# Moving the normalization's multiply and the scaled copies of v from VectorE to GpSimd in a fused attention kernel, with a branch hint, a split q evacuation and new scheduling limits

## The chip, the cores and the metric

The kernel runs on one core of one Trainium2 chip. The metric is the device time of one execution in microseconds (us), and lower is better. One run of the kernel before, 736.29 us at a granted clock of 0.85, was slow and is left out. The profile's span is about 2 us shorter than the device time. A profile is a single run, and the timed runs of one kernel spread by 0.4 to 2.9 us, so a difference of some tenths of a us between two spans means nothing by itself; verdicts rest on the timed runs. Engines are named as in the profile: PE is the matmul engine (PEld its weight loads), ACT is ScalarE, DVE is VectorE, POOL is GpSimd, SP is SyncE, which issues most DMAs. L900 is line 900 of the kernel in question; the same statement stands on another line in another kernel.

## The reference, cut to what matters

```python
# x: 2048 tokens x 512; 32 heads of 16 dimensions, everything bf16
def _A_ref(x, wqkv, wo):                       # full attention
    q, k, v = ...                              # x @ wqkv, split into heads
    p = softmax(einsum("bhqd,bhkd->bhqk", q, k) * Dh ** -0.5)
    return einsum("bhqk,bhkd->bhqd", p, v) @ wo
# _B_ref: the same with a sliding window of 8 keys, 2 apart
g = sigmoid((x * gate_w).sum(-1, keepdims=True))
return g * _A_ref(x, ...) + (1 - g) * _B_ref(x, ...)
```

The full attention dominates. Its 32 x 2048 x 2048 scores are 2048 tiles of 128 keys by 512 queries, and each tile needs one exp pass. The kernel works through 32 blocks of 64 tiles; a block is four heads by 512 queries, and its products with v collect in one PSUM bank until they are normalized, two blocks together.

## The kernel before

The exp tiles are shared by two engines. ACT takes two or three tiles at a time with its Exp function, and each of them then costs PE one product with v. DVE takes a tile with a bit trick: one `tensor_scalar` turns the scores into the bits of a 16-bit float, and two more "pieces" are shifted copies, made for up to four tiles at once. The three pieces are multiplied by v and by two scaled copies of v, so that a DVE tile costs PE three products.

```python
def exp_dve(slot_item):                                   # L1548: bits of exp, from PSUM
    (b, kt, j), bt, i, bank = slot_item
    A = SCALE * math.log2(math.e) * 1024.0
    return nc.vector.tensor_scalar(out=self.yb[bt["buf"]][:, 0, i * 512:(i + 1) * 512], in0=bank[:],
                                   scalar1=A, scalar2=1024.0 * (15.0 + PW_S[0]), op0=ALU.mult, op1=ALU.add)
def piece(bt, k):                                         # L1554: shifted copy, SBUF to SBUF
    n = len(bt["items"]) * 512
    y = self.yb[bt["buf"]]
    return nc.vector.tensor_scalar(out=y[:, k, 0:n], in0=y[:, 0, 0:n],
                            scalar1=float(round(1024.0 * (PW_S[k] - PW_S[0]))), scalar2=None, op0=ALU.add)
```

The scaled copies of v are made on DVE, out of the PSUM bank in which PE left v:

```python
def v_scaled(self, st0, nst, h0, h1, k):                  # L916
    n = (h1 - h0) * DH
    for st in range(st0, st0 + nst):
        if st in KD:                                      # the key tiles that DVE may take
            o = (st - st0) * n
            self.nc.vector.tensor_scalar(out=self.vw4[k][:, KD.index(st), h0:h1, 0:DH],
                                         in0=self.misc[:, o:o + n].rearrange("p (h e) -> p h e", e=DH),
                                         scalar1=PW_W[k], scalar2=None, op0=ALU.mult)
```

The normalization of a pair of blocks is a transpose, a reciprocal, a product with the gate, a large multiply and a transpose back, all on DVE:

```python
def n2(p0=0, n=2):                                        # L1648
    rc = self.wk.tile([P, 2, 16], F32, name="rc", tag="rc")
    t1 = self.t1[:, p0:p0 + n]
    nc.vector.reciprocal(out=rc[:, 0:n], in_=t1[:, :, :, DH])
    nc.vector.tensor_tensor(out=rc[:, 0:n], in0=rc[:, 0:n], in1=self.gA[...], op=ALU.mult)   # cut
    t2 = self.t2[(b // 2) % 2][:].rearrange("p a (r d) -> p r a d", r=2)[:, p0:p0 + n]
    return nc.vector.tensor_tensor(out=t2, in0=t1[:, :, :, 0:DH],
                            in1=rc[:, 0:n].unsqueeze(3).to_broadcast([P, n, 16, DH]), op=ALU.mult)
```

No engine's order is written by hand. A list scheduler in the kernel's own Python keeps steps with an engine, an estimated cost, dependencies, a due value and a release value. The last two count exp tiles: a step may be placed once "rel" tiles are out, and of the steps that are ready the one with the lowest "due" goes first. Tables of limits, one digit for each of 64 stretches of the 2048 tiles, tell the scheduler, for example, how much DVE may have before it is given another exp tile. The result is a fixed order of instructions on each engine. An ordinary output tile of block b is due at 64 b + 678 (dueO), the last two at 5000:

```python
def outproj_last(self, st, i, norm):                      # L1446, cut
    def ev():
        if i % 2 == 0:
            ob = self.wk.tile([P, D], BF16, name="ob", tag="ob")      # two buffers
            nc.vector.tensor_copy(out=ob[:], in_=self.misc[:])
            nc.sync.dma_start(out=self.o_dst[:, st, :], in_=ob[:])
        else:                                                         # in a tile that is idle by then
            ob = self.eg[:].bitcast(BF16)[:, 512 * (i // 2):512 * (i // 2) + 512]
            nc.scalar.copy(out=ob, in_=self.misc[:])
            nc.scalar.dma_start(out=self.o_dst[:, st, :], in_=ob)
    ch = self.chain([...four steps on PE..., (("DVE", "ACT")[i % 2], T_D1(512), ev)],
                    due=5000 + i, rel=2048 - 24, deps=[...])
```

The first scores are made by straight code, `head()`: 16 transposes of x, then q, then k, then the first scores. At the end a flag decides whether a slower exact path has to follow; with this data the branch skips it.

```python
    with ExitStack() as c1:
        _Fast(c1, tc, aps, flag).build()
    cond = nc.values_load(flag[0:1, 0:1], min_val=0, max_val=1)
    with tc.If(cond > 0):                                 # L746
        ...                                               # exact path
```

## Time and profile before

| what | before |
|---|---|
| device time, median of 3 runs | 714.45 us (714.19 to 714.62) |
| start of the profile to the first exp | 7.92 us |
| first exp to the end of the last exp | 694.5 us |
| end of the last exp to the issue of the last output | 4.55 us |
| from there to the end | 5.6 us |
| exp tiles on DVE and on ACT | 548 and 1500 |

The page of the profile gives busy time, share of the span and instructions of each engine, and the make-up of the chain of work that ended last:

```profile
PE 684.4 (96%) x8522; PEld 222.2 (31%) x8522; DVE 685.5 (96%) x1184; ACT 694.4 (97%) x702; POOL 206.0 (29%) x219
...
PE 48%; ACT 30%; DVE 9%; issue 8%; SPq 3%; DMA 2%; ACTq 0%; DVEq 0%
```

Three engines are full at once and GpSimd has room. The groups by shape show what they do: line, engine, operation, output and input by name and by shape, count, then busy time in us and the mean of one in ns, then the idle time just before them and what ended it.

```profile
L1900 ACT ACTIVATE pt<-fps 128x1024 bf16<-128x1024 f32 x564 | 546.1, 1104 | 2.8 <-PE fps L1846 2.2 <-ACT pt L1900 0.2
L1551 DVE TENSOR_SCALAR yb<-fps 128x512 int16<-128x512 f32 x548 | 355.7, 678 | 5.8 <-PE fps L1846 3.0 <-PE fps L1831 0.9
...
L1557 DVE TENSOR_SCALAR yb<-yb 128x2048 int16<-128x2048 int16 x256 | 169.8, 683 | 0.6
...
L1655 DVE TENSOR_TENSOR t<-t,rc 128x512 bf16<-128x512 f32 x15 | 10.4, 692 | 0.5
...
L922 DVE TENSOR_SCALAR vaugw<-fps 128x384 bf16<-128x384 f32 x12 | 6.3, 542 | 0.0
...
L922 DVE TENSOR_SCALAR vaugw<-fps 128x128 bf16<-128x128 f32 x12 | 3.2, 278 | 0.0
```

The last three lines are what the change takes off DVE: 15 multiplies and 24 copies, 19.9 us. The busy time by stretch (columns: stretch, us, then PE, PEld, DVE, ACT and POOL busy with instructions in brackets, granted PE clock, DMA share, GB/s) shows how full the engines are in the early part, and that GpSimd does almost nothing there:

```profile
120.00:180.00 60.00, 58.99 (x771) 18.33 (x770) 58.97 (x105) 59.46 (x62) 0.75 (x1) 1.00 0.05 15
180.00:240.00 60.00, 58.66 (x742) 17.23 (x734) 59.58 (x102) 60.00 (x62) 4.21 (x4) 1.00 0.03 7
```

The timeline (start, us, engine, instruction, count, and in brackets the idle time before it and what ended that) of the start, where the q evacuation on ACT leads to the first exp:

```profile
4.14 1.32 PE L970 MATMUL fps<-ident,x_in 128*128 128x128 bf16 x16
...
6.73 0.69 ACT L983 ACTIVATE qm<-fps,pmask 128x512 bf16<-128x512 f32 x1 [0.87 <-PE fps L885]
...
7.92 2.37 ACT L1900 ACTIVATE pt<-fps 128x1536 bf16<-128x1536 f32 x2 [0.50 <-PE fps L1846]
```

The end of the timeline, with the last projection, the last evacuation by DVE and the last output issued:

```profile
704.25 2.10 PE L885 MATMUL fps<-wAv,oT 128*32 128x512 bf16 x32
...
706.17 0.69 DVE L1460 CAST ob<-fps 128x512 bf16<-128x512 f32 x1 [1.09 <-PE fps L885]
...
707.00 0.37 ACTq L1465 DMA_DIRECT2D out_dram<-eg  x1
```

And the waits of SP's queue from 706 us on (engine, line, what for, us in total, times, longest), where L746 is the branch:

```profile
SPq L746 <- SPq L746: 3.0, 1, 3.0
```

### The profile page before, as it was taken

Reading aid. Unit: us, or ns where it says so; the run is one execution under the profiler, and the core shown is the slowest. Engines: PE = TensorE matmul, PEld = TensorE weight load, DVE = VectorE, ACT = ScalarE, POOL = GpSimd, SP = SyncE. Lnnn points to the kernel's source line nnn. Section 1 sums busy time; section 2 is a strip of 40 time slices with the busy share of each in tenths; the row PEclk is TensorE's granted clock in tenths of the full one; section 3 lists DMA queues with packets and bytes.
Section 4 is the critical chain, followed back from the end, with each engine's and each line's share of the span. In section 5 each row is a group of like instructions: output and inputs, shape, how many; then the busy total and the mean of one; then the engine's idle time right before and its main releaser. Section 6 shows DMA issues by size and latency. Waiting matters only on the chain.

```text
span 712.6 us, 21088 instructions
## 1 busy us (share of the span) xinstructions
PE 684.4 (96%) x8522; PEld 222.2 (31%) x8522; DVE 685.5 (96%) x1184; ACT 694.4 (97%) x702; POOL 206.0 (29%) x219
## 2 busy tenths in 40 slices
PE   9999999999999999999999999999999999999996
PEld 4432223323232233333222223322233332222333
DVE  6999999999999999999999999999999999999994
ACT  6999999999999999999999999999999999999994
POOL 3045000000001323322000455546555335545500
PEclk9999999999999999999999999999999999999999
DMA  6002001001000100000123437456454644636201
GB/s 172 5 15 63 10 8 25 2 3 47 3 2 13 27 2 1 10 1 13 40 64 107 123 87 167 133 130 161 124 155 106 156 107 117 158 68 177 74 21 36
DMA packets 64490, 48.71 MB, mean 68 GB/s; under 512 B 22528, under 2 KB 64000, under 8 KB 64256
## 3 DMA queue, kind: packets, MB, share of 16 engines
q1 hardware_dynamic: 63680, 45.83, 25.6%
q8 instruction: 69, 1.13, 0.7%
q0 software_dynamic: 288, 1.05, 0.4%
q10 hardware_dynamic: 416, 0.39, 0.2%
q14 instruction: 37, 0.30, 0.1%
HBM read 39.85 MB, written 5.26 MB: 63 GB/s over the span
## 4 chain that ended last, share of the span: by engine, by line
PE 48%; ACT 30%; DVE 9%; issue 8%; SPq 3%; DMA 2%; ACTq 0%; DVEq 0%
ACT pt L1900 29%; PE fps L1846 17%; PE fps L1623 15%; PE fps L885 13%; DVE yb L1551 4%; DVE yb L1557 2%; SPq L1315 1%; DMA er<-er_dram 1%; PE fps L1831 1%; PE fps L1365 1%; ACT er L1235 1%; SPq L952 1%; DMA x_in<-in_A_x_dram 1%; DVE prod L1216 0%; SPq L1341 0%
## 5 line engine op out<-in xcount | busy, mean ns | idle before, releaser
L1900 ACT ACTIVATE pt<-fps 128x1024 bf16<-128x1024 f32 (+1 forms) x688 | 688.9, 1184 | 4.0 <-PE fps L1846 3.2
L1551 DVE TENSOR_SCALAR yb<-fps 128x512 int16<-128x512 f32 x548 | 355.7, 678 | 5.8 <-PE fps L1846 3.0
L1846 PE MATMUL fps<-qm,kT 32*128 32x512 bf16 x1970 | 287.2, 383 | 17.6 <-ACT pt L1900 15.1
L1623 PE MATMUL fps<-pt,vaug 128*32 128x512 bf16 (+1 forms) x1596 | 238.1, 373 | 0.2 <-DVE kT L927 0.2
L1557 DVE TENSOR_SCALAR yb<-yb 128x2048 int16<-128x2048 int16 (+3 forms) x294 | 183.3, 647 | 0.6
L1623 PE MATMUL fps<-yb,vaugw 128*32 128x512 f16 (+1 forms) x1160 | 174.0, 372 | 0.5 <-DVE yb L1557 0.2
L1846 PEld LDWEIGHTS <-kT 32*128 32x128 bf16 x1970 | 84.6, 91 | 278.3 <-issue 272.7
L1347 POOL TENSOR_TENSOR er<-er,vw 128x512 bf16<-128x512 bf16 x64 | 73.2, 1156 | 126.8 <-DMA erb<-er_dram 65.9
L1623 PE MATMUL fps<-yb,vaug 128*32 128x512 f16 (+1 forms) x580 | 106.0, 372 | 0.1
L885 PE MATMUL fps<-xT,ww 128*32 128x512 bf16 (+2 forms) x1296 | 98.5, 380 | 0.5 <-DVE xT L973 0.2
L1623 PEld LDWEIGHTS <-vaug 128*32 128x32 bf16 x2176 | 66.9, 94 | 83.7 <-issue 75.7
L1347 POOL TENSOR_TENSOR erb<-erb,vw 128x512 bf16<-128x512 bf16 x64 | 72.9, 1156 | 66.2 <-DVE yb L1557 40.2
L1216 POOL TENSOR_TENSOR prod<-bq,bk 128x512 bf16<-128x512 bf16 x32 | 34.0, 1075 | 91.1 <-DVE prod L1216 66.8
L1623 PEld LDWEIGHTS <-vaugw 128*32 128x32 bf16 x1160 | 46.9, 95 | 36.4 <-issue 30.3
L885 PEld LDWEIGHTS <-ww 128*32 128x32 bf16 x1296 | 24.8, 95 | 33.5 <-issue 27.6
L1831 PE MATMUL fps<-qm,kz 128*32 128x512 bf16 x312 | 33.4, 384 | 0.4 <-DVE yb L1551 0.3
L1138 POOL DMA_DIRECT2D wAv<-in_A_wo_dram x1 | 0.8, 754 | 101.4 <-PE fps L1846 101.4
L1216 DVE TENSOR_TENSOR prod<-bq,bk 128x2048 bf16<-128x2048 bf16 x24 | 28.6, 1213 | 0.1
L1646 DVE STREAM_TRANSPOSE t<-fps 128x512 f32<-128x512 f32 x32 | 22.6, 705 | 2.5 <-PE fps L1623 2.5
L885 PE MATMUL fps<-woB,oB 128*32 128x512 bf16 x256 | 19.7, 382 | 0.0
L885 PE MATMUL fps<-wAv,oT 128*32 128x512 bf16 x256 | 19.3, 384 | 0.0
L1167 POOL TENSOR_TENSOR er<-xT 128x512 bf16<-128x512 bf16 x8 | 8.1, 1039 | 37.3 <-DVE yb L1557 37.3
(114 smaller groups left out, 299.0 us busy)
## 6 DMA issues: line engine op xcount, KB each, us to landing
vw<-v_dram SPq DMA_DIRECT2D x128, 128.0 KB, 3.1
er<-er_dram SPq DMA_DIRECT2D x128, 64.0 KB, 3.0
erb<-er_dram SPq DMA_DIRECT2D x128, 64.0 KB, 3.1
v_dram<-vs SPq DMA_DIRECT2D x16, 128.0 KB, 2.8
out_dram<-ob SPq DMA_DIRECT2D x15, 128.0 KB, 2.4
qm<-qs SPq DMA_DIRECT2D x112, 16.0 KB, 1.8
x_in<-in_A_x_dram SPq DMA_DIRECT2D x3, 512.0 KB, 6.4
ww<-in_B_wqkv_dram SPq DMA_DIRECT2D x12, 128.0 KB, 2.8
```

Source lines behind the costliest of these rows:

```text
L885: self.nc.tensor.matmul(out=out_ps[32 * c:32 * c + 32, 0:n], lhsT=lhsT_of(c), rhs=rhs, start=start, stop=stop, tile_position=(0, 32 * c))
L952: self.nc.sync.dma_start(out=self.qm[i % NQM][r][k:k + 16, :], in_=self.qs[i % 2][k:k + 16, :])
L1167: return nc.gpsimd.tensor_tensor(out=sq(sc, kc), in0=x, in1=x, op=ALU.mult)
L1216: return e.tensor_tensor(out=pr[m % 2][:, a:b], in0=bq[ct][:, a:b], in1=bk[ct][:, o + a:o + b], op=ALU.mult)
L1347: return nc.gpsimd.tensor_tensor(out=st_["erb"][m % 4][:, g, :], in0=st_["erb"][m % 4][:, g, :], in1=st_["vw"][m % 2][:, g, :], op=ALU.mult)
L1551: return nc.vector.tensor_scalar(out=self.yb[bt["buf"]][:, 0, i * 512:(i + 1) * 512], in0=bank[:], scalar1=A, scalar2=1024.0 * (15.0 + PW_ ...
L1557: return nc.vector.tensor_scalar(out=y[:, k, 0:n], in0=y[:, 0, 0:n], scalar1=float(round(1024.0 * (PW_S[k] - PW_S[0]))), scalar2=None, op0 ...
L1623: nc.tensor.matmul(out=out, lhsT=v, rhs=r, start=start, stop=stop, tile_position=(0, 32 * j))
L1646: nc.vector.transpose(out=self.t1[:, par].rearrange("p a b -> p (a b)"), in_=self.flex[acc[b]])
L1831: nc.tensor.matmul(out=dst[32 * c:32 * c + 32, :], lhsT=self.kz[:, j, KZ.index(kt), 32 * c:32 * c + 32], rhs=self.qm[(4 * ct + qc) % NQM][ ...
L1846: nc.tensor.matmul(out=dst, lhsT=self.kT[ct % 2][32 * j:32 * j + 32, kt * 128:(kt + 1) * 128], rhs=self.qm[(4 * ct + qc) % NQM][par][32 * ...
L1900: nc.scalar.activation(out=self.pt[pi[0]][pi[1]][:, 0:n * 512], in_=self.aslot[si][:, 0:n, :].rearrange("p a b -> p (a b)"), func=ACT.Exp, ...
```

## The change

The intent is to give DVE time back for exp tiles by moving 20 us of its work to GpSimd, to start and end a little earlier, and to refit the limits to the new balance. Cut to its core:

```diff
-TUNE = dict(R0=74, ...)
+TUNE = dict(relL=64, dueL2=2040, R0=74, ...)
 STRETCH = dict(...)          # cut: all eleven rows of limits are new
-PE_0, DVE_0, ACT_0, SLOT_0, K_0 = 1.6, 3.0, 1.75, 1.8, 2.35
+PE_0, DVE_0, ACT_0, SLOT_0, K_0 = 1.3, 2.7, 1.45, 1.5, 2.05
+T_P1 = lambda n: n / 750.0 + 0.1              # estimated cost of a scaled copy on GpSimd
@@ end of the program
+    tc.mark_branch_hint_location("exact", hint="LikelyTaken", engines=[ENG.SP, ENG.Activation, ENG.DVE, ENG.PE, ENG.Pool])
     with ExitStack() as c1:
         _Fast(c1, tc, aps, flag).build()
-    with tc.If(cond > 0):
+    with tc.If(cond > 0, label="exact"):
@@ loads
+        self.load_w("A", "q", 0)
         self.load_w("A", "k", 0)
-        self.load_w("A", "q", 0)
@@ v_scaled
-                self.nc.vector.tensor_scalar(out=self.vw4[k][...],
-                                             in0=self.misc[:, o:o + n].rearrange(...),
-                                             scalar1=PW_W[k], scalar2=None, op0=ALU.mult)
+                return self.nc.gpsimd.tensor_scalar(out=self.vw4[k][:, KD.index(st), h0:h1, 0:DH],
+                                                    in0=self.vaug4[:, st, h0:h1, 0:DH],
+                                                    scalar1=PW_W[k], scalar2=None, op0=ALU.mult)
@@ head
-                nc.scalar.activation(out=self.qm[0][0][:], in_=self.flex[1][:], func=ACT.Copy, scale=self.pmask[:, 0:1])
+                nc.scalar.activation(out=self.qm[0][0][:, 0:320], in_=self.flex[1][:, 0:320], func=ACT.Copy,
+                                     scale=self.pmask[:, 0:1])
+                nc.vector.tensor_scalar(out=self.qm[0][0][:, 320:512], in0=self.flex[1][:, 320:512],
+                                        scalar1=self.pmask[:, 0:1], scalar2=None, op0=ALU.mult)
@@ outproj_last
-                        due=5000 + i, rel=2048 - 24, deps=...)
+                        due=TUNE["dueL2"] + i, rel=2048 - TUNE["relL"], deps=...)
@@ norm_steps: n2 becomes n2a (reciprocal, gate product) on DVE and n2 on GpSimd
-                return nc.vector.tensor_tensor(out=t2, in0=t1[:, :, :, 0:DH], ...)
+                return nc.gpsimd.tensor_tensor(out=t2, in0=self.t1[:, :, :, 0:DH], ...)
```

The scaled copies now read v from SBUF, where DVE has just put it, instead of PSUM, so that the PSUM bank comes free earlier.

## The prediction

> **What bounds the kernel now.** Three engines are saturated together. The page's busy table gives ACT 694.4, DVE 685.5 and PE 684.4 of 712.6 us; the table by stretch shows ACT busy 59.5 to 60 of every 60 us from 60 to 240 us and 80 of 80 later, and DVE at 98 to 99%. The chain of waits alternates PE 48%, ACT 30%, DVE 9%. The 2048 softmax exp tiles of 128x512 are shared: 1500 on ACT, 548 on DVE; the groups give 688.9/1500 = 0.459 us a tile on ACT and (355.7 + 184.2)/548 = 0.985 us on DVE. GpSimd is busy 29%, and almost idle from 60 to 240 us.
>
> **What moves.** Off DVE: the normalization's multiply (15 at 691 ns, 10.4 us) and the scaled copies of v (24, 9.5 us). Back onto DVE: about 0.3 us of the first q evacuation. Net 19.6 us. Onto GpSimd: 15 multiplies, estimated at 1.2 us each from its 128x512 products (1040 to 1156 ns), 18 us; 24 copies, estimated at 0.3 and 0.6 us, 11 us. GpSimd goes from 206 to about 235 us.
>
> **What that is worth.** A list scheduler lays the kernel out, so freed DVE time becomes exp tiles: 19.6/(0.985 + 0.459) = 13.6 tiles, DVE 548 to about 562, ACT's exp time down 6.2 us. That lies on the critical path because ACT is never idle. Against it: a DVE tile needs three value products on PE instead of one, and PE is 98% busy before 240 us; and GpSimd's reads want the port that DVE's fast pieces use. The Trainium skill ("SBUF — State Buffer", section "Who interferes with whom") calls that pair an exclusive lock; in the waits, GpSimd's products wait 41.7 + 40.2 us for those pieces. I take off 1 us for both. Freeing PSUM banks earlier after v's evacuation, and retuned limits, give back 0.8.
>
> **Head.** The first q evacuation on ACT (0.69 us, ends 7.42) shrinks by an estimated 0.16; q's weights first may take off 0.1. First exp (7.92 us) 0.25 us earlier.
>
> **Tail.** After the last exp, PE works through 62 projection matmuls in 3.47 us without a break, while the last normalization is done at 705.1; PE's backlog sets the end. Releasing the last two tiles' projections earlier can take out up to 32: an estimated 0.7 us.
>
> **Branch hint.** The trace shows SP's compare-and-branch at 707.27 and its next instruction at 710.34, instruction fetches between; the output lands near 709.5. The Trainium skill ("Runtime: NRT & Kernel Launch", section "Instruction fetch mechanics") says a taken branch outside the window fetches its target first. If the hint prefetches, that is worth an estimated 0.8 us; at two chances in three, 0.5.
>
> **Sum.** 714.45 - 6.2 + 1.0 - 0.8 - 0.25 - 0.7 - 0.5 = 707.0 us. Range 703.5 to 710.0. Faster by over 2%: 0.03; within 2%: 0.96; slower: 0.01.
>
> **What would show it.** Right: about 562 exps on DVE; ACT near 688; DVE over 97%; no scaled copies or 691 ns multiplies on DVE; GpSimd near 235 us; first exp near 7.7; fewer than 40 projection matmuls after the last exp; SP's gap after the branch under 2.5 us. Wrong: DVE's exps unchanged with more DVE idle, PE's idle at zero in the early stretches, or DVE's pieces over 0.7 us.
>
> **What would make it wrong.** PE being the true limit, so that freed DVE time isn't used; GpSimd's multiplies over 1.5 us, holding DVE's pieces back; the retuned limits alone worth several us.

## The result, and the profile after

The ratios in this document are the mean time of one kernel's fast runs over that of the kernel before in the same rounds, with a 95% interval, so they are not quite the ratio of the medians quoted beside them.

| | median | runs | ratio to before |
|---|---|---|---|
| before, same rounds | 714.54 us (714.19 to 715.62) | 4 | |
| after | 713.98 us (713.66 to 714.64) | 4 | 0.9991 [0.9974, 1.0008] |

The prediction was 707.0 us with a range of 703.5 to 710.0, and 713.98 lies outside. The page after:

```profile
PE 689.5 (97%) x8558; PEld 221.9 (31%) x8558; DVE 678.4 (95%) x1154; ACT 691.3 (97%) x698; POOL 243.3 (34%) x258
...
PE 44%; ACT 36%; issue 9%; DVE 6%; DMA 3%; SPq 1%; POOL 0%; ACTq 0%; DVEq 0%; POOLq 0%
```

The work did move: DVE is 7.1 us less busy and GpSimd 37.3 us more. But less busy is not what was predicted; DVE was to be filled up again with exp tiles and to stay over 97% busy, and it is at 95%. The groups by shape:

```profile
L1912 ACT ACTIVATE pt<-fps 128x1024 bf16<-128x1024 f32 x560 | 540.8, 1094 | 2.9 <-PE fps L1858 2.2 <-ACT pt L1912 0.2
...
L1559 DVE TENSOR_SCALAR yb<-fps 128x512 int16<-128x512 f32 x556 | 360.4, 681 | 7.0 <-PE fps L1858 5.0 <-PE fps L1843 0.2
...
L1565 DVE TENSOR_SCALAR yb<-yb 128x2048 int16<-128x2048 int16 x258 | 171.7, 687 | 0.4
...
L1664 POOL TENSOR_TENSOR t<-t,rc 128x512 bf16<-128x512 f32 x15 | 15.9, 1059 | 121.1 <-DVE yb L1565 95.9 <-DVE rc L1659 16.7 <-DVE prod L1224 8.4
...
L922 POOL TENSOR_SCALAR vaugw<-vaug 128x384 bf16<-128x384 bf16 x12 | 14.3, 1195 | 40.1 <-PE fps L887 22.3 <-DVE vaug L915 17.1
...
L922 POOL TENSOR_SCALAR vaugw<-vaug 128x128 bf16<-128x128 bf16 x12 | 6.6, 550 | 20.9 <-DVE vaug L915 14.7 <-DVE yb L1565 5.7
```

DVE has 556 exp tiles instead of 548, so 8 more, where 13.6 were predicted. The same two early stretches:

```profile
120.00:180.00 60.00, 59.88 (x802) 18.89 (x794) 57.24 (x98) 59.91 (x62) 13.81 (x12) 1.00 0.04 12
180.00:240.00 60.00, 59.90 (x767) 17.71 (x765) 57.71 (x97) 60.00 (x63) 5.23 (x5) 1.00 0.04 10
```

PE is now busy for 59.9 of every 60 us, and DVE, which had been the fuller of the two in the second stretch, is at 57.7. DVE's waits from 140 to 230 us, first before, then after, name PE:

```profile
DVE qs L935 <- PE fps L885: 0.3, 1, 0.3
```

```profile
DVE yb L1559 <- PE fps L1858: 1.2, 5, 0.3
DVE vaug L915 <- PE fps L887: 1.1, 2, 0.5
DVE bk L1200 <- PE fps L887: 1.0, 1, 1.0
DVE bq L1200 <- PE fps L887: 0.7, 1, 0.7
```

The start of the timeline after. The first exp comes at 9.16 us instead of 7.92:

```profile
5.02 1.35 PE L978 MATMUL fps<-ident,x_in 128*128 128x128 bf16 x16 [0.35 <-DMA x_in<-in_A_x_dram]
...
7.49 0.53 ACT L991 ACTIVATE qm<-fps,pmask 128x320 bf16<-128x320 f32 x1 [0.71 <-PE fps L887]
...
8.05 0.42 DVE L993 TENSOR_SCALAR qm<-fps,pmask 128x192 bf16<-128x192 f32 x1 [1.21 <-ACT qm L991]
...
9.16 1.45 ACT L1912 ACTIVATE pt<-fps 128x1536 bf16<-128x1536 f32 x1 [1.15 <-DVE kT L995]
```

The end after. The last exp ends at 700.80 us, 1.65 us earlier than before (702.45), but the last output is issued at 708.54, which is 1.54 us later:

```profile
703.56 1.91 PE L887 MATMUL fps<-wAv,oT 128*32 128x512 bf16 x32
704.23 0.69 DVE L1449 CAST ob<-fps 128x512 bf16<-128x512 f32 x1 [0.57 <-PE fps L887]
704.88 0.69 DVE L1468 CAST ob<-fps 128x512 bf16<-128x512 f32 x1
...
707.83 0.69 DVE L1449 CAST ob<-fps 128x512 bf16<-128x512 f32 x1 [2.25 <-DMA out_dram<-ob]
708.54 0.33 SPq L1450 DMA_DIRECT2D out_dram<-ob  x1
```

The last evacuation waits 2.25 us for a DMA: both buffers named "ob" are still being sent. SP's wait at the branch (L748 here) is much shorter:

```profile
SPq L748 <- SPq L748: 1.2, 2, 0.7
```

Cut at the first exp, the last exp and the last issue of an output, the two profiles compare with the prediction like this. The predicted column sorts the terms of its sum; the middle is 6.2 - 1.0 + 0.8.

| stretch | before | after | change | predicted |
|---|---|---|---|---|
| start to first exp | 7.92 | 9.16 | +1.24 | -0.25 |
| first exp to last exp | 694.5 | 691.6 | -2.9 | -6.0 |
| last exp to last output issued | 4.55 | 7.74 | +3.2 | -0.7 |
| last output issued to end | 5.6 | 3.84 | -1.8 | -0.5 |
| sum | 712.6 | 712.4 | -0.2 | -7.45 |

Two large questions follow. Why did the end get 3.2 us longer? And why is the middle worth 2.9 us instead of 6.0?

### The profile page after: what moved, and what is told of

Same layout as the page of the kernel before. It is cut to its first block, busy times and chain, and to the rows that moved or that the text cites. A ratio compares the mean times of both kernels' runs of the same rounds, so it can differ in the third digit from the quotient of the medians.

```text
span 712.4 us, 21197 instructions
## 1 busy us (share of the span) xinstructions
PE 689.5 (97%) x8558; PEld 221.9 (31%) x8558; DVE 678.4 (95%) x1154; ACT 691.3 (97%) x698; POOL 243.3 (34%) x258
## 3 DMA queue, kind: packets, MB, share of 16 engines
q8 instruction: 68, 1.11, 0.7%
## 4 chain that ended last, share of the span: by engine, by line
PE 44%; ACT 36%; issue 9%; DVE 6%; DMA 3%; SPq 1%; POOL 0%; ACTq 0%; DVEq 0%; POOLq 0%
ACT pt L1912 35%; PE fps L1858 16%; PE fps L1631 15%; PE fps L887 10%; DVE yb L1559 3%; DVE yb L1565 2%; PE fps L1843 1%; PE fps L1373 1%; DMA erb<-er_dram 1%; PE fps L1238 1%; SPq L1349 1%; ACT er L1243 1%; DMA x_in<-in_A_x_dram 1%; DMA ww<-in_A_wqkv_dram 0%; SPq L1323 0%
## 5 line engine op out<-in xcount | busy, mean ns | idle before, releaser
L1912 ACT ACTIVATE pt<-fps 128x1024 bf16<-128x1024 f32 (+1 forms) x684 | 686.1, 1172 | 4.7 <-PE fps L1858 2.2
L1559 DVE TENSOR_SCALAR yb<-fps 128x512 int16<-128x512 f32 x556 | 360.4, 681 | 7.0 <-PE fps L1858 5.0
L1631 PE MATMUL fps<-pt,vaug 128*32 128x512 bf16 (+1 forms) x1588 | 241.0, 373 | 0.1
L1565 DVE TENSOR_SCALAR yb<-yb 128x2048 int16<-128x2048 int16 (+2 forms) x294 | 187.4, 662 | 0.5
L1631 PE MATMUL fps<-yb,vaug 128*32 128x512 f16 (+1 forms) x588 | 108.6, 372 | 0.0
L1631 PEld LDWEIGHTS <-vaug 128*32 128x32 bf16 x2176 | 65.2, 94 | 83.4 <-issue 75.1
L1631 PEld LDWEIGHTS <-vaugw 128*32 128x32 bf16 x1176 | 47.1, 95 | 40.2 <-issue 33.2
L1664 POOL TENSOR_TENSOR t<-t,rc 128x512 bf16<-128x512 f32 x15 | 15.9, 1059 | 121.1 <-DVE yb L1565 95.9
L922 POOL TENSOR_SCALAR vaugw<-vaug 128x128 bf16<-128x128 bf16 (+1 forms) x24 | 20.9, 872 | 61.0 <-DVE vaug L915 31.8
L1843 PE MATMUL fps<-qm,kz 128*32 128x512 bf16 x344 | 37.8, 383 | 0.2 <-DVE yb L1559 0.2
```

Of the source, the lines that this page charges most:

```text
L922: return self.nc.gpsimd.tensor_scalar(out=self.vw4[k][:, KD.index(st), h0:h1, 0:DH], in0=self.vaug4[:, st, h0:h1, 0:DH], scalar1=PW_W[k], ...
L1631: nc.tensor.matmul(out=out, lhsT=v, rhs=r, start=start, stop=stop, tile_position=(0, 32 * j))
L1664: return nc.gpsimd.tensor_tensor(out=t2, in0=self.t1[:, :, :, 0:DH], in1=h["rc"][:].unsqueeze(3).to_broadcast([P, 2, 16, DH]), op=ALU.mult)
L1843: nc.tensor.matmul(out=dst[32 * c:32 * c + 32, :], lhsT=self.kz[:, j, KZ.index(kt), 32 * c:32 * c + 32], rhs=self.qm[(4 * ct + qc) % NQM][ ...
L1912: nc.scalar.activation(out=self.pt[pi[0]][pi[1]][:, 0:n * 512], in_=self.aslot[si][:, 0:n, :].rearrange("p a b -> p (a b)"), func=ACT.Exp, ...
```

## The experiments

My theory after the result was that the end lost time by the new due value of the last two output tiles, that the start lost it by the hint and by the split evacuation, and that the middle fell short because PE, not DVE, limits the early part. The main rivals were that an earlier release helps and the loss has another cause, that GpSimd's work disturbs DVE through the port they share, and that the refit tables alone made the middle. The scheduler's five starting estimates (PE_0 and the others) changed too, and no run takes them back alone. Eighteen kernels were run, each with four or five timed runs.

### The end: a_tail and a_obfree

In a_tail the two values of the last output tiles are put back:

```diff
-TUNE = dict(relL=64, dueL2=2040, R0=74, ...)
+TUNE = dict(relL=24, dueL2=5000, R0=74, ...)
```

> The changed kernel with the last two output tiles' release and due values put back (24 and 5000 in place of 64 and 2040); all that comes before the last 64 exp tiles is the same. Theory: with a due of 2040 these tiles overtake two ordinary output tiles (due 2534), whose evacuation on DVE at 707.83 then waited 2.25 us for one of two output buffers; put back, no evacuation waits for a buffer, the last output is issued within 4.7 us of the last exp (it was 7.7 us, before 4.6), and the time falls by 2.0 to 3.5 us, to about 711. Rival: the tail is long because DVE ran dry or PE's backlog grew; then the time stays within 0.7 us of 714.0.

Measured: 711.70 us (711.33 to 712.06), ratio 0.9956 [0.9943, 0.997]. That is 2.3 us less than after, and the intervals of the two ratios don't overlap. Up to about 683 us ACT and DVE have the order of after; from there on it differs, and DVE has 554 exp tiles instead of 556. A build with only the release value changed (relL=64, dueL2=5000) comes out as the same program as a_tail, so the release value does nothing by itself. The two work together, though: a build with only the due value changed (24 and 2040) comes out in a third order, which was not run. The end of a_tail's timeline:

```profile
703.72 0.69 DVE L1468 CAST ob<-fps 128x512 bf16<-128x512 f32 x1 [0.51 <-PE fps L887]
...
704.44 0.33 SPq L1469 DMA_DIRECT2D out_dram<-ob  x1
704.55 0.38 ACTq L1473 DMA_DIRECT2D out_dram<-eg  x1
```

The last output is issued at 704.55 us, 4.0 us before that of after, while the last exp ends at about the same time (700.59 and 700.80). The due values explain the order. Block 29's four ordinary output tiles are due at 64 x 29 + 678 = 2534. With 5000 the last two tiles go behind them; with 2040 they go ahead, and ordinary tiles are left for the very end. Counted in the trace, PE has 64 output-projection matmuls after the last exp in the kernel before, 72 in after and 49 in a_tail. The time saved, 2.3 us, is less than the 4.0 us at the issue, because in this profile a_tail's last outputs took 3.6 and 3.8 us to land, and the very last one of after 2.0.

The theory was that the wait for an "ob" buffer makes the loss, and the rival that the order does. In a_obfree the order of after is kept, and one of the last two tiles goes to the unused half of another tile instead of an "ob" buffer:

```diff
             if i % 2 == 0:
-                ob = self.wk.tile([P, D], BF16, name="ob", tag="ob")
-                nc.vector.tensor_copy(out=ob[:], in_=self.misc[:])
-                nc.sync.dma_start(out=self.o_dst[:, st, :], in_=ob[:])
+                ob = self.eg[:].bitcast(BF16)[:, 512:1024]
+                nc.vector.tensor_copy(out=ob, in_=self.misc[:])
+                nc.sync.dma_start(out=self.o_dst[:, st, :], in_=ob)
```

> The changed kernel, with one of the last two output tiles evacuated to an idle half of another tile in place of the second output buffer; every instruction keeps its place and engine. Theory (the wait for the buffer is the loss): DVE's last evacuation no longer waits for an output's landing (it stood idle 2.25 us for it), the last output is issued 2 us or more earlier, and the time falls by 1.8 to 2.5 us to 711.5 to 712.2. Rival (the order of the last tiles costs of itself): it falls by less than 1 us.

Measured: 712.70 us (712.17 to 712.88), ratio 0.9972 [0.9958, 0.9986]. All instructions kept their places. The end of its timeline:

```profile
704.42 0.69 DVE L1468 CAST eg<-fps 128x512 bf16<-128x512 f32 x1
...
705.07 0.69 DVE L1449 CAST ob<-fps 128x512 bf16<-128x512 f32 x1
...
705.79 0.59 SPq L1450 DMA_DIRECT2D out_dram<-ob  x1
```

The wait is gone and the last issue moves from 708.54 to 705.79 us, of which 0.45 is an earlier last exp. The time falls by 1.3 us of the 2.3. In the profiles the stretch from the last exp to the last issue is 7.7 us in after, 5.4 in a_obfree and 4.0 in a_tail, so 2.3 of 3.8 us are the wait for a buffer, and the rest is the order, with 72 projection matmuls and four evacuations after the last exp instead of 49 and two. Both readings give the wait somewhat over half. By the timed runs alone that split isn't firm: the intervals of a_obfree and a_tail overlap, and other runs with a_tail's end took 711.6 to 712.4 us (c_again, d_hintlate and c_both, below).

### The start: a_head and a_kfirst

In a_head the first q evacuation is on ACT alone again; in a_kfirst the weights of k are loaded first again:

```diff
 # a_head
-                nc.scalar.activation(out=self.qm[0][0][:, 0:320], in_=self.flex[1][:, 0:320], func=ACT.Copy,
-                                     scale=self.pmask[:, 0:1])
-                nc.vector.tensor_scalar(out=self.qm[0][0][:, 320:512], in0=self.flex[1][:, 320:512],
-                                        scalar1=self.pmask[:, 0:1], scalar2=None, op0=ALU.mult)
+                nc.scalar.activation(out=self.qm[0][0][:], in_=self.flex[1][:], func=ACT.Copy, scale=self.pmask[:, 0:1])
 # a_kfirst
-        self.load_w("A", "q", 0)
         self.load_w("A", "k", 0)
+        self.load_w("A", "q", 0)
```

> The changed kernel with the first q evacuation on ACT alone, as before; nothing else differs. Theory: DVE's part waited for ACT's part of the same tile (1.21 us to 8.05), so the split is run one after the other and pushes the first k evacuation and the first exp back; undone, the first exp comes 0.3 to 0.5 us earlier relative to the first transposes (it was 4.14 us after them, before 3.78), and the time falls by 0.3 to 0.5 us. Rival: the whole 1.24 us lost at the head is a later landing of x; then the interval from transposes to first exp stays above 4.05 us and the time stays.

> The changed kernel with k's weights loaded before q's, as before. Theory: both are issued after x and PE starts on q's projections when x's copies are done, so the order is worth nothing: within 0.2 us of 714.0, first exp within 0.2 us relative to the first transposes. Rival: q's weights were late before, so k first costs 0.2 us or more; or the order is what delayed x, so k first gives up to 0.9 us.

Measured: a_head 714.04 us (713.74 to 714.48), ratio 0.9990 [0.9976, 1.0003]; a_kfirst 714.19 us (714.15 to 714.80), ratio 0.9995 [0.9982, 1.0009]. Neither changes the time. But a_head's start is earlier:

```profile
7.16 0.69 ACT L991 ACTIVATE qm<-fps,pmask 128x512 bf16<-128x512 f32 x1 [0.71 <-PE fps L887]
7.38 0.29 DVE L992 CAST kT<-fps 128x128 bf16<-128x128 f32 x1 [0.88 <-PE fps L887]
...
8.36 2.37 ACT L1909 ACTIVATE pt<-fps 128x1536 bf16<-128x1536 f32 x2 [0.51 <-PE fps L1855]
```

In after, DVE's part of the split tile started at 8.05 us, after ACT's part had ended at 8.01, with [1.21 <-ACT qm L991] as its wait: the two halves ran one after the other, and DVE's evacuation of k, which leads to the first scores, queued behind them. It is the program that does this: in the trace DVE's part waits for the semaphore that ACT's part raises. The 16 transposes took between 1.07 and 1.89 us in the profiles, and the trace shows with what that goes: PE's granted clock reaches its full value at 4.0 us in a_head, 5.7 in after and 7.1 in c_norm_dve, and transposes start some 107 ns apart before that moment and 55 ns after it (before and a_nohint have a wait of some 0.3 us for x in between besides). Among profiles in which they took the same time (1.07 to 1.12 us), the first exp came 3.38 to 3.40 us after the first transpose without the split (a_head, b_hint and three more) and 3.85 to 3.91 us with it (a_tail, a_kfirst, a_obfree). So the split costs 0.5 us at the start, where an estimated 0.16 was to be gained. It doesn't reach the end: what is lost at the start is swallowed in the fixed order that follows.

### The hint: a_nohint, b_hint and d_hintlate

In a_nohint the hint is taken out of after, in b_hint it is put alone into the kernel before, and d_hintlate is a_tail with the hint marked just before the scheduled part:

```diff
 # a_nohint; b_hint is the same edit, added to the kernel before
-    tc.mark_branch_hint_location("exact", hint="LikelyTaken", engines=[ENG.SP, ENG.Activation, ENG.DVE, ENG.PE, ENG.Pool])
-    with tc.If(cond > 0, label="exact"):
+    with tc.If(cond > 0):
 # d_hintlate
             self.jobs()
+            self.tc.mark_branch_hint_location("exact", hint="LikelyTaken", engines=[...])
             self.run()
```

> The changed kernel without the branch hint. Theory: the hint saves the fetch after the branch (SP 0.5 us from branch to next instruction with it, 3.0 without), worth about 0.5 to 1.2 us at the end, and costs 0.1 us at the start; without it the time rises by 0.4 to 1.1 us. Rival A: it is worth nothing since the output's landing covers the fetch: within 0.2 us. Rival B: the hint's register writes delay SP's first loads (its first packet at 2.82 us, before 1.84), so that without it the first transposes start at 4.1 in place of 5.0 and the time falls by up to 0.8 us.

> The kernel before with the branch hint added and nothing else. Theory: net of its later first loads it gains 0.4 to 1.3 us, as in the changed kernel; SP's gap after its branch falls from 3.0 to 0.5 us and the first transposes come 0.6 to 0.9 us later. Rival: with an undisturbed tail the later start costs as much as the end gains; within 0.3 us.

> The changed kernel with the tail's priorities put back (711.7), and the branch hint's register writes moved from the program's first instructions to behind the head, after the first loads are issued. Theory: at the start the hint holds SP's first loads back (its first packet at 2.3 to 3.0 us in four profiles with it, 1.84 in two without; first transposes 4.9 to 5.1 against 4.1 to 4.2), while its gain at the end needs only that it stands well before the branch; moved, the transposes start near 4.2, SP's gap after its branch stays near 0.5 us, and the time falls by 0.5 to 0.8 us to about 711.0. Rival: the head's shift is swallowed later, or the hint no longer holds at the branch: 711.5 or more.

Measured: a_nohint 715.04 us (714.52 to 715.62), ratio 1.0005 [0.9991, 1.0018], 1.06 us more than after. b_hint 713.66 us (713.34 to 714.15), ratio 0.9985 [0.9971, 0.9999], 1.2 us less than the 714.84 us of before in its rounds. The two agree: the hint is worth about 1.1 us, though each is little more than the spread of one kernel's runs. SP's wait at the branch in a_nohint is back:

```profile
SPq L747 <- SPq L747: 2.8, 1, 2.8
```

From the compare-and-branch to SP's next instruction the trace records show 3.07 us before, 2.85 in a_nohint and 0.52 in after and in b_hint. That is 2.5 us, of which less than half arrives. After the branch the traces have six instruction packets of 8 KB in before and in a_nohint, and two in after and three in b_hint, which fits the reading as a fetch. The records of b_hint show one reason why less arrives: SP gets through its first five semaphore instructions and then stands until 710.03 us in the one that has to wait for the outputs, the first of which lands at 710.01 us, so that the end is now set by their landing. And the hint costs something at the start. Each engine executes it there, as one instruction (BRANCH_PREFETCH_HINT, where the expectations speak of register writes), in 50 to 60 ns at 0.70 to 0.82 us, and SP's first load sends its first packet at 2.25 to 2.96 us in all 17 profiles with the hint, and at 1.84 us in all three without (before, a_nohint, b_newlim); the first transposes start at 4.89 to 5.11 us instead of 4.14 to 4.38. ACT's queue, which carries the other half of the first x tile, is earlier in exchange: its first packet comes at 1.93 to 1.98 us in 16 of the 17, and at 2.26 to 2.58 without. So the two queues change places, rather than both being late. Why 50 ns of hint make SP's loads 0.4 to 1.1 us late isn't shown, and neither is how much of it reaches the end: in b_hint the first exp starts 0.39 us later than before and the last ends only 0.09 us later.

d_hintlate is a miss. It took 712.17 us (711.50 to 712.43), ratio 0.9963 [0.9949, 0.9977], but its hint instructions came out at the same place, at the start, with the same order of instructions on ACT, DVE, GpSimd and SP as a_tail. It is a second measurement of a_tail (711.70 us), and whether a later hint would keep the gain without the cost stays open.

### The middle: the two moves, undone in a fixed order

For the middle, a base with a clean start and end was needed, so c_both has a_tail's and a_head's edits together; it was run again with later kernels as c_again.

> The changed kernel with the tail's priorities and the first q evacuation both put back. Theory: with no evacuation waiting for an output buffer, the 0.5 us that the q evacuation gained at the head (first exp 3.38 us after the first transposes, 4.14 before) is no longer swallowed at the end; the time is 0.3 to 0.6 us under the run with the tail alone put back (711.7), about 711.2. Rival: the head's gain is lost in the middle, where the static order waits anyway; then it stays within 0.15 us of 711.7.

> c_both once more, the control of the three runs beside it: 711.7 to 712.5 us.

Measured: c_both 712.43 us (711.68 to 713.75), ratio 0.9971 [0.9957, 0.9984]; c_again, the same kernel, 711.62 us (711.37 to 712.46), ratio 0.9957 [0.9943, 0.9971]. The two differ by 0.8 us, which is about how far such a difference can be trusted. Against a_tail's 711.70 us, undoing the split gains nothing once more.

Then three kernels that change the engine or the size of the moved work and leave the scheduled order as it is:

```diff
 # c_norm_dve: the multiply back on DVE, at its place in the order
-                return nc.gpsimd.tensor_tensor(out=t2, in0=self.t1[:, :, :, 0:DH],
+                return nc.vector.tensor_tensor(out=t2, in0=self.t1[:, :, :, 0:DH],
 # c_v_dve: the scaled copies back on DVE, still read from SBUF
-                return self.nc.gpsimd.tensor_scalar(out=self.vw4[k][:, KD.index(st), h0:h1, 0:DH],
+                return self.nc.vector.tensor_scalar(out=self.vw4[k][:, KD.index(st), h0:h1, 0:DH],
 # c_norm_short: one of 16 columns multiplied, wrong on purpose; the rest of t2 set to 0 once
-                return nc.gpsimd.tensor_tensor(out=t2, in0=self.t1[:, :, :, 0:DH],
-                                               in1=h["rc"][:].unsqueeze(3).to_broadcast([P, 2, 16, DH]), op=ALU.mult)
+                return nc.gpsimd.tensor_tensor(out=t2[:, :, :, 0:1], in0=self.t1[:, :, :, 0:1],
+                                               in1=h["rc"][:].unsqueeze(3), op=ALU.mult)
```

> c_both with the normalization's 15 multiplies issued to DVE at the very places where GpSimd had them; the layout of everything else, all limits and all tiles stay (554 exps on DVE). It adds 10.4 us to DVE. Theory (DVE's time is on the critical path at those places): the time rises by 6 to 10 us over c_both. Rival (DVE has slack there, PE or ACT limits): it rises by less than 3 us, and then moving these multiplies could not have gained more than that.

> c_both with the 24 scaled copies of v issued to DVE at the places where GpSimd had them, layout and limits kept. It adds about 9 us to DVE, nearly all before 170 us. The same two readings: a rise of 6 to 9 us over c_both if DVE is critical there, under 3 us if PE limits that stretch (PE's matmul groups start 96% back to back from 60 to 240 us).

> Wrong result on purpose: c_both with the 15 multiplies on GpSimd cut to one column in sixteen (1.06 us to some 0.2 us), layout kept. If GpSimd's hold on the shared port or its lateness cost the middle its expected gain, the time falls by 1 us or more under c_both; if GpSimd is harmless, it stays within 0.4 us.

Measured, with c_both in the same rounds:

| kernel | median | ratio to before | against c_both |
|---|---|---|---|
| c_norm_dve | 720.35 us (718.90 to 721.18) | 1.0070 [1.0056, 1.0084] | +7.9 us |
| c_v_dve | 712.45 us (711.96 to 713.71) | 0.9971 [0.9958, 0.9985] | 0.0 us |
| c_norm_short (wrong result) | 712.42 us (711.22 to 713.02) | 0.9965 [0.9951, 0.9979] | 0.0 us |

The moved groups in c_norm_dve:

```profile
L1661 DVE TENSOR_TENSOR t<-t,rc 128x512 bf16<-128x512 f32 x15 | 13.6, 905 | 0.0
```

and in c_v_dve:

```profile
L922 DVE TENSOR_SCALAR vaugw<-vaug 128x384 bf16<-128x384 bf16 x12 | 3.0, 250 | 0.0
...
L922 DVE TENSOR_SCALAR vaugw<-vaug 128x128 bf16<-128x128 bf16 x12 | 1.8, 180 | 0.0
```

The multiply matters in this order: 13.6 us put back on DVE cost 7.9 us by the medians and 7.1 by the ratios. It also takes 905 ns there in the mean and not 692, and nothing in c_norm_dve keeps GpSimd still while it runs, as the old order did. The Trainium skill ("SBUF — State Buffer", section "Who interferes with whom") says that a DVE instruction with two SBUF inputs contends with a GpSimd instruction that reads SBUF. The trace agrees: the seven multiplies with no tensor work on GpSimd beside them took 679 to 683 ns, and of the eight with some, seven took 734 to 1318.

The copies, put back, cost nothing. The experiment is weaker than it was meant to be: I had counted on some 9 us, and from SBUF the copies took only 250 and 180 ns, 4.8 us in all, against 542 and 278 ns from PSUM in the kernel before. The Trainium skill ("VectorE: DVE Perf Modes", section "Mode 4×_2P — both tricks at once") gives four elements a cycle for this mode, and the section after it ("What auto-detection actually checks") asks for 16-bit tensors, a single source, and source and destination in SBUF; the durations agree: between 128 and 384 columns a copy grows by 0.27 ns a column from SBUF and by 1.03 from PSUM. So about half of the copies' price on DVE was the price of reading them as f32 from PSUM and not as bf16 from SBUF; type and place changed together, so their parts aren't separated.

c_norm_short takes 15 multiplies on GpSimd from 1056 to 341 ns, so 10.7 us off GpSimd, and gains nothing. GpSimd's multiplies don't hold anything up at the size they have. About the port it says little, because DVE's pieces overlap tensor work on GpSimd for 8.7 us in it as in c_again. In c_v_dve, which takes 20.9 us of copies off GpSimd, that overlap falls to 6.0 us and nothing is gained, but there DVE has 4.8 us more to do. The two together speak against the rival of a disturbed port, and don't exclude it.

### The middle: which engine limits it

c_bproj_half takes 256 matmuls, an estimated 13.8 us, off PE alone, in the early part, by leaving out half of the contraction of the sliding branch's q and k. s_act takes 8 of 512 columns off every exp on ACT, s_dve 16 of 512 off every exp on DVE, s_both does both. All four were wrong and still passed the tolerance.

```diff
 # c_bproj_half
-    self.proj_mm(self.w_tiles[("B", kind, ct)], (0, 1), sc)),
+    self.proj_mm(self.w_tiles[("B", kind, ct)], (0,), sc)),
-    self.proj_mm(self.w_tiles[("B", kind, ct)], (2, 3), sc)),
+    self.proj_mm(self.w_tiles[("B", kind, ct)], (3,), sc)),
 # s_act (cut): out[:, 0:n * 512] and in_[:, 0:n, :] become [:, :, 0:504] of each 512, the rest set to 1 once
-    in_=self.aslot[si][:, 0:n, :].rearrange("p a b -> p (a b)"),
+    in_=self.aslot[si][:, 0:n, 0:504],
 # s_dve (cut): the rest of yb set to a constant once
-    out=self.yb[bt["buf"]][:, 0, i * 512:(i + 1) * 512], in0=bank[:],
+    out=self.yb[bt["buf"]][:, 0, i * 512:i * 512 + 496], in0=bank[:, 0:496],
```

> Wrong result on purpose: c_both (712.4) with half the contraction left out of branch B's q and k projections, layout kept. It takes 256 matmuls, about 13.8 us of PE, out of the stretch from 35 to 230 us, where PE's groups are 96% back to back, and nothing from other engines. Theory (PE limits that stretch, so DVE's freed time could not be used there, and adding 8 us of copies to DVE cost nothing): the first 640 exp tiles are done 3 us or more earlier than in c_both (228.4 us) and the time falls by 3 us or more. Rival (ACT or DVE limits): less than 1 us.

> Wrong result on purpose: c_both with ACT's exps cut from 512 to 504 columns a tile, layout kept; 8 columns at the 0.427 us that 512 of them add (triple 1331 less pair 904 ns) are 6.7 ns a tile, 10.0 us on 1494 tiles. The prediction's assumption (ACT is never idle, so its time is the time): the time falls by 8 to 10 us. Rival (three engines bind together): it falls by 2 to 5 us.

> Wrong result on purpose: c_both with DVE's exps cut from 512 to 496 columns, layout kept: an estimated 16.7 ns on 554 tiles, 9.2 us. If ACT alone limits: within 0.5 us of the control. If they bind together: it falls by 1 to 4 us.

> Wrong result on purpose: both cuts at once, 10 us off ACT and 9 us off DVE. If ACT alone limits: as s_act. If ACT and DVE bind together and PE has room: it falls by more than s_act and s_dve together, 7 us or more. If PE then limits: little more than the larger of the two.

| kernel | taken away | median | ratio to before | gain over c_again |
|---|---|---|---|---|
| c_bproj_half | 13.8 us of PE (estimate) | 710.58 us (710.30 to 712.12) | 0.9947 [0.9933, 0.996] | 1.0 us |
| s_act | 10.3 us of ACT | 705.86 us (705.59 to 706.37) | 0.9876 [0.986, 0.9891] | 5.8 us |
| s_dve | 8.9 us of DVE | 711.33 us (711.15 to 711.83) | 0.9951 [0.9937, 0.9966] | 0.3 us |
| s_both | both | 705.62 us (705.24 to 705.96) | 0.9872 [0.9856, 0.9887] | 6.0 us |

What was taken away is worked out from the spacing of back-to-back instructions: on ACT 904 to 890 ns for a pair and 1331 to 1310 ns for a triple, on DVE 598 to 582 ns for a tile. (c_bproj_half ran in other rounds than c_again; against c_both its gain is 1.85 us.) Of ACT's time 0.56 of each us arrives. Of DVE's 0.03 arrives, less than the spread of c_both and c_again. So in this order ACT limits most of the time, and DVE has nothing more to give: its idle time grows from 20.6 us in c_again to 25.7 in s_dve, and its waits for scores from PE before its exps from 5.4 to 7.8. PE by itself gives a little: in c_bproj_half the first 640 tiles are done at 227.0 us instead of 228.4, where my theory asked for 3 us or more. Above all, DVE's idle time from 140 to 230 us, in which it waits for PE, is 4.3 us in it and 4.4 in c_both. So my theory that PE's early load is what holds the middle back is not borne out, and why DVE waits there stays open.

These are values in a fixed order, though, and for time taken away; time added to DVE did cost, as c_norm_dve showed. A scheduler that lays the kernel out anew turns DVE's freed time into other exp tiles, and no experiment here shows what that is worth with the best tables for it.

### The tables: a_oldlim and b_newlim

a_oldlim is after with the limits of before; b_newlim is before with the limits of after:

```diff
 STRETCH = dict(
-    backlog="0333323133333333033333345336335333336333333333343333344333334633",
+    backlog="3333333333333333333633333333433363534333333336633333333333334336",
     ...                                                  # all eleven rows exchanged
 )
```

> The changed kernel with the old tables of limits. Theory: the tables are fitted to one layout of work and do not carry over; with the wrong ones the layout gives DVE far fewer exps (536 in place of 556) and the time rises by 12 to 25 us. Rival: the new tables are a small part of the change; within 4 us.

> The kernel before with the new tables of limits and nothing else. The same: fitted to another layout, they give DVE 517 exps in place of 548 and cost 12 to 25 us; if the new tables were good in themselves, the time would fall instead.

Measured: a_oldlim 729.78 us (727.79 to 730.65), ratio 1.0202 [1.0186, 1.0218]; b_newlim 732.54 us (731.80 to 732.74), ratio 1.0246 [1.0231, 1.0262]. DVE gets 536 and 517 exp tiles in them. Each set of tables fits one layout and costs the other 2% or more, some 16 to 18 us, about twice the 7.45 us that the whole change was predicted to bring. So the part of the tables can't be had by exchanging them: how much of the middle's 2.9 us comes from the moves and how much from the refit stays open.

### The version that beats both

a_tail (711.70 and, as d_hintlate, 712.17 us) and c_both (712.43 and 711.62 us) are faster than both kernels, with ratios of 0.9956 to 0.9971 whose intervals all lie below 1.

## Why the prediction was wrong

**The tail was wrong in sign, and in the profiles it is the largest single term.** The step that failed: "PE's backlog sets the end. Releasing the last two tiles' projections earlier can take out up to 32: an estimated 0.7 us." The release value does nothing by itself (a build with it alone is the same program as a_tail), and with the due value beside it the order turned round. After the last exp there were 72 projection matmuls, not "fewer than 40", and before there had been 64. PE's backlog then no longer set the end: the last matmul was done at 705.48 us, and the last evacuation began only at 707.83, because it had waited 2.25 us for a buffer. Measured in the profiles, +3.2 us instead of -0.7; measured by a_tail, 2.3 us of the time. I had read what the change releases, and not what it is put ahead of: 2040 against the 2534 of four other tiles was in the code.

**The middle had the right mechanism and the wrong size.** The step: "freed DVE time becomes exp tiles: 19.6/(0.985 + 0.459) = 13.6 tiles, DVE 548 to about 562, ACT's exp time down 6.2 us." It became 8 tiles. The page shows ACT's exps at 688.9 us before and 686.1 after, 2.8 us less. From the spacing of ACT's exps, 3.6 us come from fewer tiles in another mix of pairs and triples, and 0.7 us are given back in longer waits: -2.9. What became of DVE's freed time, in us, counted in the trace without overlap over tiles 1 to 2048:

```text
multiplies and scaled copies taken off          -18.3
exps, 548 to 556 tiles                           +6.5
pieces (294 in both)                             +3.6
output evacuations moved behind the last exp     -1.0
all else                                         +0.2
idle, 13.6 to 19.7                               +6.1
the interval itself, 693.1 to 690.2              -2.9
```

So 10.1 us of the freed time went into exps and pieces, and 6.1 us into new idle time. 3.6 of that idle is between about 140 and 230 us, where PE is busy 59.9 of 60 us and DVE waits for it, and 2.7 is in the last 128 tiles. The profile looks like the warning in the prediction that DVE may find PE full, to which I gave, with GpSimd's port, 1 us. The experiment doesn't bear it out: in c_bproj_half, which relieves PE, that idle time stays, and the gain is only 1.0 to 1.85 us. What is shown is that DVE stands idle and that, by s_dve, time taken off it is worth next to nothing in this order; what makes it wait is open. "That lies on the critical path because ACT is never idle" is right for ACT's time, at 0.56 for 1 (s_act). It was DVE's time that couldn't be exchanged for it at the full rate.

The time at which a number of tiles was done shows where the 2.9 us were won (own count from the traces, us):

```text
tiles done      before     after     c_v_dve   c_again
   8             12.02     12.98      13.13     12.98
 384            143.84    140.70     141.32    140.68
 640            230.31    228.40     229.12    228.38
1920            658.56    656.80     657.36    656.64
2048            702.45    700.80     701.79    701.07
```

All of it and more comes in the first 384 tiles, where after has 105 exps on DVE and before 97. From 384 to 640 it gives 1.2 us back, with no more DVE tiles than before (66 and 68), and after that the two run level. It is tempting to say that the copies, most of which lie in the early part, made the gain; c_v_dve, with the copies on DVE, is only 0.6 us later than c_again at 384 tiles, so little of the gain hangs on which engine makes the copies once they are read from SBUF. How far the tables made the new order, and the gain with it, stays open.

**The allowance for DVE's waits and the port was too small.** The Trainium skill's exclusive lock ("SBUF — State Buffer", section "Who interferes with whom") shows: the part of DVE's pieces that overlaps tensor work on GpSimd grew from 4.5 to 8.9 us, and of the 16 pieces of two tiles in after, the three that overlap such work took 762 ns in the mean and the others 418. All pieces together grew longer by some 2.3 us by their means. The 1 us taken off for both was 1 us of the whole time, which at the prediction's own rate (6.2 us for 19.6) is some 3.2 us of DVE's. Against that stand 2.3 us of longer pieces and 6.1 us of new idle time, so it was the idle time, and not the port alone, that broke the allowance. GpSimd stood long behind the pieces (95.9 us before its multiplies, and the 41.7 + 40.2 us that the prediction took as a sign of the lock), but these are waits that the kernel itself puts in: its `run()` makes each GpSimd step depend on the last DVE step marked `port`. GpSimd's own time is not scarce, as c_norm_short shows.

**The head was wrong in sign.** The step: "The first q evacuation on ACT (0.69 us, ends 7.42) shrinks by an estimated 0.16". ACT's part did shrink to 0.53 us. But DVE's part waited for it, and the first exp came 0.5 us later for that, and some 0.7 to 0.9 later for the late loads that came with the hint. Neither a_head nor a_kfirst gained time, so the split's part and the order of the loads didn't reach the total.

**The hint was right in mechanism and near in size.** The Trainium skill ("Runtime: NRT & Kernel Launch", section "Instruction fetch mechanics") led to the reading that the 3.07 us after the branch are a fetch, and with the hint they are 0.52. "worth an estimated 0.8 us; at two chances in three, 0.5" was measured as 1.1 us net, in both directions. The prediction saw that the landing of the outputs caps it; it didn't see the cost at the start.

**GpSimd's load was right for the multiply and wrong for the copies.** 1.2 us were estimated for a multiply and 1059 ns measured, near the 2.6 cycles an element of the Trainium skill ("GPSIMD Engine Reference", section "3.1 Elementwise — side-by-side cycle accounting"; with the 1.2 GHz of that page an estimate of 1.11 us). The copies were estimated at 0.6 and 0.3 us and took 1195 and 550 ns. 243 us in all instead of 235 did no harm.

The four stretches add up: 3.1 us too much expected of the middle, 1.5 of the head, 3.9 of the tail, and 1.3 too little of the end after the last output, together 7.2 us, which is the distance between 707.0 and the 714.17 us of the profiled run.

## What to carry to other kernels

A change of a priority is to be read against the priorities of everything it now overtakes, and a tail against the number of its buffers; here that was worth a third of a per cent, and undoing one line gave the best version. Time freed on one of three full engines is worth what the other two can take up: removing 8.9 us from DVE gave 0.3 us and removing 10.3 us from ACT gave 5.8, so measure each engine's exchange rate by shortening its work before counting on one. Limits fitted to a layout belong to it: exchanged, they cost 2%, so a change and its refit can't be judged apart by exchanging tables.

## What the Trainium skill lacked or had wrong

- "Runtime: NRT & Kernel Launch" tells of the stall after a taken branch, but no page that I found tells of a hint that fetches the target early. Here it took SP's gap from 3.07 to 0.52 us, cost 50 to 60 ns on each engine at the start, came with SP's first loads 0.4 to 1.1 us later, and was worth 1.1 us net.
- "GPSIMD Engine Reference", section "3.1 Elementwise — side-by-side cycle accounting", gives about 1.8 cycles an element as the best case of a tight loop, and no figure for a built-in operation with one input. The scaled copies (one input, bf16, SBUF to SBUF, in groups of 16 columns) took 1195 ns for 384 columns and 550 ns for 128; the slope between the two is 2.5 ns an element, which is 3.0 cycles at 1.2 GHz.
- "SBUF — State Buffer" says who contends with whom, but gives no size for work that overlaps only now and then. Here, 15 multiplies on DVE went from 692 to 905 ns in the mean when nothing kept GpSimd's work apart from them; seven of them had no such work beside them and stayed at 679 to 683 ns.
